# Attention and two feed-forward layers on one core: conversions of weights spread over the steps, the split of x moved to ScalarE and VectorE, the last tiles sent in halves

## The chip, the cores and the metric

The kernel runs on one core of one Trainium2 chip. The metric is the device time of one execution, in microseconds (us). The engines are named as in the profile: PE (TensorE, matmuls) with PEld (its weight loads), DVE (VectorE), ACT (ScalarE), POOL (GpSimd) and SP (SyncE, which here only issues DMAs).

## What is computed

Rotary attention, then a feed-forward layer with g = h - tanh(h), then a gated one without a nonlinearity. All arithmetic of the reference is float32 (the weights reach the chip as 64-bit numbers).

```
attn  = softmax(scale * rot(q) @ rot(k)^T) @ v      # 4 x 8 heads, 576 rows, 64 wide
x     = attn.transpose(0, 2, 1, 3).reshape(2304, 512)
h     = x @ w_in                                    # 512 -> 2048
x2    = (h - tanh(h)) @ w_out                       # 2048 -> 512
a, b  = x2 @ w1, x2 @ w2                            # 512 -> 1024
out   = ((a * b) @ w3) @ w_o2                       # 1024 -> 1024 -> 512
```

## The kernel before

**Precision.** Each operand of a matmul is kept as two parts of a 32-bit type, hi and lo; a product is three matmuls (hi·hi, hi·lo, lo·hi). To *split* a tile is one copy that makes hi and one subtraction that makes lo.

**Stages.** Attention fills the first 296 us, by an order written out as tables of numbers; it is the same before and after. Then the tokens are five blocks of columns: four of 512 and block 4, the *narrow block*, of 256 (the last 64 rows of each of the four sequences). The first feed-forward layer runs in two *halves* of 40 steps (296 to about 750 us): half 0 with hidden columns 0 to 1023, half 1 with the rest, each over the blocks in the order 0, 1, 2, 4, 3, with 8 steps (of 128 hidden columns) per block. Step n issues `emit_h(n+2)` (12 matmuls, x times w_in, L808), `emit_g(n+2)` (g = h - tanh h and its split: ScalarE L821 to L824 and L831, VectorE L825 to L828 and L832), `emit_x2(n)` (12 matmuls into the four x2p accumulators, L846), and then `do(n)`, which performs what a table has put into that step. The last phase (about 750 to 1052 us, `emit_ab` and `emit_out`) makes a·b and multiplies it by w3·w_o2, a product of weights alone.

**Side work in the steps.** The table is filled with `at(step, function)` (L920) and holds, for each half:

- *conversions*: `next_conv` / `to_f32` (L253) turns the next raw 64-bit tile into float32 with two operations on ScalarE (L264, L266) and two on VectorE (L267, L269), and then `next_load` sends SP for another raw tile. The raw pool has two buffers, the z tiles that take the result three. The order of the tiles is the list `units`.
- *placing*: `place` splits a converted tile into its slot (copy on ScalarE L276, subtraction on VectorE L277). A slot is free for the next half's weights only in the last block of the current half (`last`).
- *the folded product*: `conv_o2`, then per 128 rows `wp_trans` (four transposes of w3 on TensorE, and a split) and `wp_mm` (12 matmuls), eight times per half; results go to DRAM (`wp_dram`) and in half 1 come back in a tile `wpe` to be added and split.
- FOLD_AT, FOLD_EVERY, EARLY_EVERY and LATE_EVERY (L177 to L181) say in which steps these stand. EARLY = 4 conversions of the next half's weights are done ahead of its last block, into one tile z_early.

**The split of x.** `split_x` (L774) splits the next block's x on GpSimd, chunk kc by chunk (copy L776, subtraction L777), and stores it to DRAM, whence half 1 loads it (`load_x`, the xl tiles). In half 0 it is called in the last three steps of a block, for the block that follows; at the end of half 1 and in the last phase for x2, the input of that phase (key '3').

**The tail.** After the last block of the last phase two tiles ot of 128x512 are copied from PSUM, one by ScalarE, one by VectorE, and leave in two DMAs each, all issued by SP.

## Time and profile before

| | us |
|---|---|
| median of 3 runs (lowest, highest) | 1060.43 (1058.98, 1061.11) |
| the profiled execution's own time | 1059.08 |
| span of its profile | 1057.3 |
| TensorE busy in it | 1028.3 |
| VectorE, ScalarE, GpSimd busy | 707.9, 610.5, 286.5 |
| mean granted clock of TensorE, of full speed | 0.996 |

The span is what the trace covers of the profiled execution; the execution's own time is 1.8 us longer. A row of a timeline gives the start and the duration of an instruction (or of a run of like ones, xN); in brackets stands the idle time of the engine just before it and what ended it. "L846" is line 846 of the kernel before. A tile's name stands without its number: g, s_out (a slot with w_out), xs (split x), z and raw (converted and raw weights).

### The profile page before, as it was taken

The page shows a single profiled execution, that of the slowest core. Times are in us where ns is not written, and L with a number is a line of the kernel's source. Part 1 is how long each engine was busy: PE and PEld are TensorE (multiplying, and loading weights), DVE is VectorE, ACT ScalarE, POOL GpSimd, SP SyncE. Part 2 cuts the span into 40 slices and gives each one's busy share as a digit, 9 for nine tenths or more (in the row PEclk, how much of TensorE's full clock was granted, in tenths as well). Part 3 has the DMA queues.
Part 4 walks back from the last instruction along what each step waited for, and adds up shares of the span by engine and source line. Part 5 has one row for each costly group of instructions (what it writes and reads, how often), then busy time and mean ns, then how long its engine had stood idle before and what let it go on. Part 6 is the DMA issues. An engine that isn't in the chain of part 4 may idle for free.

```text
span 1057.3 us, 15775 instructions
## 1 busy us (share of the span) xinstructions
PE 1028.3 (97%) x5568; PEld 847.2 (80%) x5568; DVE 707.9 (67%) x1367; ACT 610.5 (58%) x1285; POOL 286.5 (27%) x332
## 2 busy tenths in 40 slices
PE   6989999999999999999999999999999999999998
PEld 5777777777767788888888888898788888888887
DVE  7889999999669866669999776769863212112121
ACT  4779888898767655468888655557652111111111
POOL 3667777777543021111000000040101103020000
PEclk9999999999999999999999999999999999999999
DMA  5658787876444313136335112523630101001010
GB/s 165 158 138 195 180 184 186 185 192 157 88 160 160 100 60 110 40 120 219 108 132 179 60 60 100 168 95 107 239 120 1 40 1 40 1 1 40 1 40 20
DMA packets 71327, 114.99 MB, mean 109 GB/s; under 512 B 12241, under 2 KB 42961, under 8 KB 71249
## 3 DMA queue, kind: packets, MB, share of 16 engines
q1 hardware_dynamic: 71248, 113.99, 37.2%
q8 instruction: 44, 0.72, 0.3%
q14 instruction: 35, 0.28, 0.1%
HBM read 67.96 MB, written 20.45 MB: 84 GB/s over the span
## 4 chain that ended last, share of the span: by engine, by line
PE 82%; DVE 7%; DMA 5%; ACT 3%; issue 2%; POOL 0%; SPq 0%; DVEq 0%; POOLq 0%; ACTq 0%
PE pw L988 19%; PE x2p L846 16%; PE h L808 14%; PE o L1047 9%; PE sc L501 8%; PE pv L597 5%; PE te L556 5%; PE wp L893 4%; DMA qs<-qp 2%; DMA raw_w<-in_moe_w 1%; PE pv L594 1%; PE te L559 1%; DMA q<-in_q 1%; DVE g L832 1%; DMA raw_in<-in_moe_w_in 1%
## 5 line engine op out<-in xcount | busy, mean ns | idle before, releaser
L846 PE MATMUL x2p<-g,s_out 128*128 128x512 f32 (+1 forms) x960 | 216.8, 374 | 7.5 <-DVE g L832 4.6
L846 PEld LDWEIGHTS x2p<-g,s_out 128*128 128x128 f32 x960 | 170.2, 191 | 42.4 <-DVE g L832 7.7
L994 DVE TENSOR_TENSOR ab<-a,pw 128x512 f32<-128x512 f32 (+1 forms) x40 | 25.4, 634 | 173.5 <-PE pw L988 173.5
L528 POOL TENSOR_SCALAR e<-e,r 128x576 f32<-128x576 f32 x144 | 113.4, 799 | 47.4 <-DVE r L524 29.1
L511 ACT ACTIVATE e<-sc,nm 128x576 f32<-128x576 f32 x144 | 107.7, 748 | 28.7 <-DVE nm L506 25.7
L506 DVE TENSOR_REDUCE nm<-sc 128x1 f32<-128x576 f32 x144 | 106.6, 749 | 12.9 <-PE sc L501 11.5
L808 PE MATMUL h<-xl,s_in 128*128 128x512 f32 (+1 forms) x480 | 105.9, 369 | 0.0
L1047 PE MATMUL o<-wpt,abs 128*128 128x512 f32 x432 | 104.5, 390 | 0.0
L808 PEld LDWEIGHTS h<-xl,s_in 128*128 128x128 f32 x480 | 84.0, 188 | 15.2
L501 PE MATMUL sc<-ks,qs 128*128 128x288 f32 x480 | 90.8, 316 | 4.6 <-DMA qs<-qp 3.2
L1047 PEld LDWEIGHTS o<-wpt,abs 128*128 128x128 f32 x432 | 80.6, 188 | 16.4
L825 DVE TENSOR_TENSOR g_s<-g_s,h 128x512 f32<-128x512 f32 (+1 forms) x80 | 50.6, 633 | 59.8 <-ACT g_m L824 59.7
L992 ACT COPY a<-pw 128x512 f32<-128x512 f32 (+1 forms) x40 | 21.7, 543 | 112.8 <-PE pw L988 112.8
L501 PEld LDWEIGHTS sc<-ks,qs 128*128 128x128 f32 x480 | 67.2, 188 | 22.2 <-issue 10.9
L556 PE MATMUL te<-ident,e 128*128 128x128 f32 x576 | 83.8, 277 | 0.6 <-POOL e L528 0.5
L831 ACT CAST g<-g_q 128x512 fp32r<-128x512 f32 (+1 forms) x80 | 46.1, 576 | 51.2 <-DVE g_q L828 50.7
L996 ACT CAST abs<-ab 128x512 fp32r<-128x512 f32 (+1 forms) x40 | 23.1, 577 | 85.5 <-DVE ab L994 85.5
L821 ACT ACTIVATE g_s<-h 128x512 f32<-128x512 f32 (+1 forms) x80 | 44.0, 550 | 49.1 <-PE h L808 48.7
L556 PEld LDWEIGHTS te<-ident,e 128*128 128x128 f32 x576 | 68.8, 143 | 3.5 <-POOL e L528 1.7
L905 POOL TENSOR_TENSOR wpe<-wpe 128x512 fp32r<-128x512 f32 x8 | 10.7, 1335 | 215.4 <-ACT wpe L904 215.4
L832 DVE TENSOR_TENSOR g<-g_q,g 128x512 fp32r<-128x512 f32 (+1 forms) x80 | 55.0, 688 | 19.9 <-ACT g L831 19.5
L828 DVE COPY_PREDICATED g_q<-g_m,g_t 128x512 f32<-128x512 int32 (+1 forms) x80 | 57.0, 713 | 0.9
(299 smaller groups left out, 2119.3 us busy)
## 6 DMA issues: line engine op xcount, KB each, us to landing
ks<-kp SPq DMA_DIRECT2D x60, 288.0 KB, 4.1
raw_w<-in_moe_w SPq DMA_DIRECT2D x32, 512.0 KB, 3.8
raw_in<-in_moe_w_in SPq DMA_DIRECT2D x16, 512.0 KB, 3.8
raw_out<-in_moe_w_out SPq DMA_DIRECT2D x16, 512.0 KB, 3.6
xl<-xs_dram SPq DMA_DIRECT2D x16, 512.0 KB, 5.8
qs<-qp SPq DMA_DIRECT2D x60, 128.0 KB, 3.5
wp_dram<-wpe SPq DMA_DIRECT2D x24, 256.0 KB, 2.0
k<-in_k SPq DMA_DIRECT2D x16, 256.0 KB, 4.2
```

Source lines behind the costliest of these rows:

```text
L501: nc.tensor.matmul(s[:, n, 0:HS], lhs, rhs, start=t == 0, stop=t == len(terms) - 1)
L506: nc.vector.tensor_reduce(d["nm"][:, j:j + 1], d["ss"][j][:, :, 0:HS], AX.XY, ALU.max, negate=True)
L511: nc.scalar.activation(d["e"][:, j, :].rearrange("p (n s) -> p n s", n=2), d["ss"][j][:, :, 0:HS], AF.Exp, bias=d["nm"][:, j:j + 1], accum ...
L528: nc.gpsimd.tensor_scalar(d["e"][:, j, :], d["e"][:, j, :], d["r"][:, j:j + 1], 1.0, ALU.mult, ALU.mult)
L556: nc.tensor.transpose(ps[:, n * 128:(n + 1) * 128], e[:, o + n * 128:o + (n + 1) * 128], ident)
L597: nc.tensor.matmul(ps[64 * j:64 * j + 64, 0:n], vt[:, j, m, :], et[j][:, m, :], start=False, stop=m == NQ - 1, skip_group_check=True)
L808: nc.tensor.matmul(ps[:, 0:w], ws[:, a, kk], x[:, b_, 0:w], start=kc == 0 and t == 0, stop=kc == NK - 1 and t == 2)
L828: nc.vector.copy_predicated(qq, mk.bitcast(I32), t)
L832: nc.vector.tensor_tensor(g[:, 1, 0:w], qq, f32(g[:, 0, 0:w]), ALU.subtract))
L846: nc.tensor.matmul(x2ps[j][o][:, 0:w], ws[:, a, oo], g[:, b_, 0:w], start=c == 0 and t == 0, stop=c == HF - 1 and t == 2)
L988: nc.tensor.matmul(ps[:, 0:w], ws[:, a, kk], x[:, b_, 0:w], start=kc == 0 and t == 0, stop=kc == NK - 1 and t == 2)
L1047: nc.tensor.matmul(outps[j][t], g[:, a, tt], wp[c][:, b_, :], start=c == 0 and i == 0, stop=c == NF2 - 1 and i == 2)
```

## The change

Three things are changed (the three tiles of half 0 that attention leaves unconverted keep their steps 0, 1, 2, though the line that sets them reads otherwise).

1. **Where conversions stand.** `room` gives each step of a half a weight (its block's width, less at the ends of the half) and `spread` deals the conversions of o2 and w3 and the first twelve of the next half's weights evenly over that weight, over blocks 0 to 3 in order (all steps but the last eight). The order of `units` changes with it: the next half's first four stand between the w3 tiles. EARLY is 12 in place of 4: the early tiles wait in x tiles that are no longer read (`early_z`). The last four are converted one step ahead of their placing. In half 1 the tile wpe moves from the buffer of x2 to that of xt (block 4).
2. **split_x** has the copy on ScalarE and the subtraction on VectorE, but for block 0 of half 0 and, in the last phase, blocks 1 to 4, which stay on GpSimd.
3. **The tail**: each of the last two tiles is copied by halves, the left by ScalarE, the right by VectorE, and the second DMA of each is issued by ScalarE.

```diff
-FOLD_AT, FOLD_EVERY = (3, 10), 2.25
-EARLY_EVERY, LATE_EVERY = 2, (0.5, 1)
-EARLY = 4
+CONV_FROM = (2, 1)
+EARLY = 12
...
-    units = half1 + fold[0] + half2 + fold[1] + half3
+    units, work = list(half1), []
+    for i, half in enumerate((half2, half3)):
+        o2u, w3u = fold[i][:NF2 // 2], fold[i][NF2 // 2:]
+        mix = [("o2", r) for r in range(NF2 // 2)]
+        n = 0
+        for f in range(NF2):
+            mix.append(("w3", f))
+            if f < 4:
+                mix.append(("next", n))
+                n += 1
+        mix += [("next", c) for c in range(n, len(half))]
+        work.append(mix)
+        for kd, c in mix:
+            units.append(dict(o2=o2u, w3=w3u, next=half)[kd][c])
...
+    def early_z(hf, i):
+        r, c = divmod(i, 4)
+        if (hf, r) not in early:
+            if hf == 0:
+                early[hf, r] = xpool.tile([128, 4, 512], I32, tag=f"x{r}", name=f"ze0_{r}")
+            elif r == 0:
+                early[hf, r] = xpool.tile([128, 4, 512], I32, tag="x2", name="ze1_0")
+            else:
+                early[hf, r] = xpool.tile([128, 4, 512], I32, tag=f"x{r - 1}", name=f"ze1_{r}")
+        return early[hf, r][:, c]
...
-        nc.gpsimd.tensor_scalar(t[:, 0, 0:w], src[:, kc, :], 1.0, 1.0, ALU.mult, ALU.mult)
-        nc.gpsimd.tensor_tensor(t[:, 1, 0:w], src[:, kc, :], f32(t[:, 0, 0:w]), ALU.subtract)
+        if key[0] == "3" and key[1] or key == (0, 0):
+            nc.gpsimd.tensor_scalar(t[:, 0, 0:w], src[:, kc, :], 1.0, 1.0, ALU.mult, ALU.mult)
+            nc.gpsimd.tensor_tensor(t[:, 1, 0:w], src[:, kc, :], f32(t[:, 0, 0:w]), ALU.subtract)
+        else:
+            nc.scalar.copy(t[:, 0, 0:w], src[:, kc, :])
+            nc.vector.tensor_tensor(t[:, 1, 0:w], src[:, kc, :], f32(t[:, 0, 0:w]), ALU.subtract)
...
-            t = xpool.tile([128, 2, 512], F32, tag="x2", name=f"wpe_{i}{f}")
+            t = xpool.tile([128, 2, 512], F32, tag="xt", name=f"wpe_{i}{f}")
...
+    def room(hf, i):
+        p, c = divmod(i, HF)
+        if hf == 0:
+            r = {0: 0.5, HF - 3: 0.6, HF - 2: 0.6, HF - 1: 0.3}.get(c, 1.0)
+        else:
+            r = {0: 0.5, HF - 1: 0.5}.get(c, 1.0)
+        return r * widths[order[p]] / SM
...
+        n_even = NK + NF2 + EARLY
+        steps = spread(hf, CONV_FROM[hf], H2 - HF, n_even)
+        k = w3_at = 0
+        for m, (kd, c) in enumerate(work[hf]):
+            k = max(k, b0 + steps[m]) if m < n_even else None
+            if kd == "w3":
+                w3_at = k = max(k, w3_at + 1)
+            if kd == "o2":
+                at(k, conv_o2, hf, c)
+            elif kd == "w3":
+                at(k, conv_z, None)
+                at(k + 1, wp_trans, hf, c)
+                at(k + 2, wp_mm, hf, c)
             else:
...
+                if c < EARLY:
+                    at(k, conv_z, lambda hf=hf, c=c: early_z(hf, c))
+                else:
+                    at(last + c // 2 - 1, conv_z, None)
+                at(last + c // 2, place, next_half[c])
...
-                if t % 2:
+                if n == len(seq3) - 1:
+                    nc.scalar.copy(o[:, 0:DM // 2], outps[j][t][:, 0:DM // 2])
+                    nc.vector.tensor_copy(o[:, DM // 2:], outps[j][t][:, DM // 2:])
+                elif t % 2:
...
-                        nc.sync.dma_start(out[bb * S + SM:(bb + 1) * S, :],
-                                          o[64 * r:64 * r + 64, :])
+                        queue = nc.scalar if r else nc.sync
+                        queue.dma_start(out[bb * S + SM:(bb + 1) * S, :],
+                                        o[64 * r:64 * r + 64, :])
```

How the instructions stand on VectorE, at three places. (Line numbers of the changed kernel: L265 and L267 are the conversion, L275 the placing, L805 the subtraction of split_x, L853 to L856 and L860 the chain of g, L884 the addition to x2.)

**First place**: VectorE at the start of half 0, between attention's last row and the first g. Before:

```order
L578 COPY ett1_3_3_4417<-te2_79_4435 128x128
L267 SCALAR_TENSOR_TENSOR z_out6_4582<-z_out6_4582,raw_out6_3738 128x512
L269 SCALAR_TENSOR_TENSOR z_out6_4582<-raw_out6_3738,z_out6_4582 128x512
L267 SCALAR_TENSOR_TENSOR z_in7_4632<-z_in7_4632,raw_in7_4002 128x512
L269 SCALAR_TENSOR_TENSOR z_in7_4632<-raw_in7_4002,z_in7_4632 128x512
L277 TENSOR_TENSOR s_out6_4589<-z_out6_4582,s_out6_4589 128x512
L277 TENSOR_TENSOR s_in7_4639<-z_in7_4632,s_in7_4639 128x512
L825 TENSOR_TENSOR g_s_0_4495<-g_s_0_4495,h_0_4482 128x512
```

After:

```order
L576 COPY ett1_3_3_4417<-te2_79_4435 128x128
L265 SCALAR_TENSOR_TENSOR z_out6_4582<-z_out6_4582,raw_out6_3738 128x512
L267 SCALAR_TENSOR_TENSOR z_out6_4582<-raw_out6_3738,z_out6_4582 128x512
L265 SCALAR_TENSOR_TENSOR z_in7_4632<-z_in7_4632,raw_in7_4002 128x512
L805 TENSOR_TENSOR xs_(0, 1)_0_4730<-x1_1548,xs_(0, 1)_0_4730 128x512
L275 TENSOR_TENSOR s_out6_4589<-z_out6_4582,s_out6_4589 128x512
L267 SCALAR_TENSOR_TENSOR z_in7_4632<-raw_in7_4002,z_in7_4632 128x512
L805 TENSOR_TENSOR xs_(0, 1)_1_4783<-x1_1548,xs_(0, 1)_1_4783 128x512
L853 TENSOR_TENSOR g_s_0_4495<-g_s_0_4495,h_0_4482 128x512
```

The conversions and splits are the same but for the last split (s_in7), which has gone behind the first operations on g; the two subtractions of split_x for block 1 (chunks 0 and 1) stand among them.

**Second place**: VectorE in the narrow block of half 0, step 26's g. Before:

```order
L825 TENSOR_TENSOR g_s_26_5886<-g_s_26_5886,h_26_5873 128x256
L827 TENSOR_TENSOR g_t_26_5888<-h_26_5873,g_t_26_5888 128x256
L826 SCALAR_TENSOR_TENSOR g_q_26_5887<-g_q_26_5887,g_s_26_5886 128x256
L267 SCALAR_TENSOR_TENSOR z_early0_5973<-z_early0_5973,raw_in8_5699 128x512
L828 COPY_PREDICATED g_q_26_5887<-g_m_26_5889,g_t_26_5888 128x256
L269 SCALAR_TENSOR_TENSOR z_early0_5973<-raw_in8_5699,z_early0_5973 128x512
L854 COPY x22_5860<-x2p3_16_5451 128x512
L832 TENSOR_TENSOR g_26_5898<-g_q_26_5887,g_26_5898 128x256
```

After:

```order
L853 TENSOR_TENSOR g_s_26_5952<-g_s_26_5952,h_26_5939 128x256
L855 TENSOR_TENSOR g_t_26_5954<-h_26_5939,g_t_26_5954 128x256
L854 SCALAR_TENSOR_TENSOR g_q_26_5953<-g_q_26_5953,g_s_26_5952 128x256
L856 COPY_PREDICATED g_q_26_5953<-g_m_26_5955,g_t_26_5954 128x256
L860 TENSOR_TENSOR g_26_5964<-g_q_26_5953,g_26_5964 128x256
```

The conversion into z_early and the copy of x2 have left the chain of g, which stands alone.

**Third place**: VectorE in the narrow block of half 1, step 66's g. Before:

```order
L825 TENSOR_TENSOR g_s_66_7939<-g_s_66_7939,h_66_7926 128x256
L827 TENSOR_TENSOR g_t_66_7941<-h_66_7926,g_t_66_7941 128x256
L826 SCALAR_TENSOR_TENSOR g_q_66_7940<-g_q_66_7940,g_s_66_7939 128x256
L881 TENSOR_TENSOR w3t_14_7975<-tw3_14_7970,w3t_14_7975 128x512
L828 COPY_PREDICATED g_q_66_7940<-g_m_66_7942,g_t_66_7941 128x256
L267 SCALAR_TENSOR_TENSOR z_w315_8268<-z_w315_8268,raw_w315_8043 128x512
L269 SCALAR_TENSOR_TENSOR z_w315_8268<-raw_w315_8043,z_w315_8268 128x512
L832 TENSOR_TENSOR g_66_7951<-g_q_66_7940,g_66_7951 128x256
```

After:

```order
L860 TENSOR_TENSOR g_65_8077<-g_q_65_8066,g_65_8077 128x256
L884 TENSOR_TENSOR x22_5934<-x2p3_56_7658,x22_5934 128x512
L265 SCALAR_TENSOR_TENSOR ze1_2_8103<-ze1_2_8103,raw_w14_8004 128x512
L853 TENSOR_TENSOR g_s_66_8123<-g_s_66_8123,h_66_8110 128x256
L267 SCALAR_TENSOR_TENSOR ze1_2_8103<-raw_w14_8004,ze1_2_8103 128x512
L854 SCALAR_TENSOR_TENSOR g_q_66_8124<-g_q_66_8124,g_s_66_8123 128x256
L855 TENSOR_TENSOR g_t_66_8125<-h_66_8110,g_t_66_8125 128x256
L265 SCALAR_TENSOR_TENSOR ze1_2_8103<-ze1_2_8103,raw_w24_8050 128x512
L856 COPY_PREDICATED g_q_66_8124<-g_m_66_8126,g_t_66_8125 128x256
L267 SCALAR_TENSOR_TENSOR ze1_2_8103<-raw_w24_8050,ze1_2_8103 128x512
L860 TENSOR_TENSOR g_66_8135<-g_q_66_8124,g_66_8135 128x256
```

The split of the transposed w3 and the conversion of a w3 tile are gone; two conversions of the last phase's weights into a waiting tile (ze1_2) stand in the chain, and the additions to x2 around it.

## Rows read from the trace of the kernel before

**Rows 1.** The page, part 1: busy us (share of span) xinstructions
```profile
PE 1028.3 (97%) x5568; PEld 847.2 (80%) x5568; DVE 707.9 (67%) x1367; ACT 610.5 (58%) x1285; POOL 286.5 (27%) x332
```

**Rows 2.** Busy us by stretch: PE, PEld, DVE, ACT, POOL; PEclk, DMA share, GB/s
```profile
296.00:350.00 54.00, 48.59 (x194) 38.05 (x193) 48.22 (x65) 39.63 (x70) 17.09 (x14) 0.94 0.46 160
475.00:500.00 25.00, 23.83 (x146) 20.68 (x145) 23.30 (x46) 20.40 (x45) 4.50 (x4) 1.00 0.69 233
500.00:725.00 225.00, 225.00 (x1100) 190.32 (x1099) 182.96 (x304) 152.74 (x282) 19.10 (x16) 1.00 0.33 111
```

**Rows 3.** PE's timeline: start, us, engine line op out<-in xcount [idle <-releaser]
```profile
308.76 4.61 PE L846 MATMUL x2p<-g,s_out 128*128 128x512 f32 x12 [2.01 <-ACT g L831]
...
314.82 2.88 PE L846 MATMUL x2p<-g,s_out 128*128 128x512 f32 x12
...
336.18 0.39 PE L846 MATMUL x2p<-g,s_out 128*128 128x512 f32 x1
337.31 2.81 PE L846 MATMUL x2p<-g,s_out 128*128 128x512 f32 x11 [0.74 <-DVE g L832]
...
343.61 0.51 PE L846 MATMUL x2p<-g,s_out 128*128 128x512 f32 x1 [0.78 <-ACT g L831]
...
345.93 4.38 PE L846 MATMUL x2p<-g,s_out 128*128 128x512 f32 x11 [1.81 <-DVE g L832]
...
483.46 1.58 PE L846 MATMUL x2p<-g,s_out 128*128 128x256 f32 x11 [0.86 <-DVE g L832]
...
748.54 2.83 PE L846 MATMUL x2p<-g,s_out 128*128 128x512 f32 x11 [0.74 <-DVE g L832]
```

**Rows 4.** DVE's timeline, same columns
```profile
300.84 1.66 DVE L269 SCALAR_TENSOR_TENSOR z_in<-raw_in,z_in 128x512 int32<-128x512 int32 x1
302.43 1.78 DVE L277 TENSOR_TENSOR s_out<-z_out,s_out 128x512 fp32r<-128x512 f32 x1
304.13 0.68 DVE L277 TENSOR_TENSOR s_in<-z_in,s_in 128x512 fp32r<-128x512 f32 x1
...
345.19 0.68 DVE L832 TENSOR_TENSOR g<-g_q,g 128x512 fp32r<-128x512 f32 x1
345.79 0.68 DVE L825 TENSOR_TENSOR g_s<-g_s,h 128x512 f32<-128x512 f32 x1
...
483.33 0.41 DVE L825 TENSOR_TENSOR g_s<-g_s,h 128x256 f32<-128x256 f32 x1
483.66 0.41 DVE L827 TENSOR_TENSOR g_t<-h,g_t 128x256 f32<-128x256 f32 x1
```

**Rows 5.** POOL's timeline, the splits of x
```profile
301.92 1.74 POOL L777 TENSOR_TENSOR xs_(0, 1)_1_4774<-x,xs_(0, 1)_1_4774 128x512 fp32r<-128x512 f32 x1
...
335.10 1.61 POOL L777 TENSOR_TENSOR xs_(0, 1)_2_4827<-x,xs_(0, 1)_2_4827 128x512 fp32r<-128x512 f32 x1
...
342.39 1.60 POOL L777 TENSOR_TENSOR xs_(0, 2)_1_5216<-x,xs_(0, 2)_1_5216 128x512 fp32r<-128x512 f32 x1
...
482.09 1.05 POOL L776 TENSOR_SCALAR xs_(0, 3)_3_6146<-x 128x512 fp32r<-128x512 f32 x1
...
746.33 1.61 POOL L777 TENSOR_TENSOR xs_('3', 1)_0_9082<-x,xs_('3', 1)_0_9082 128x512 fp32r<-128x512 f32 x1
```

**Rows 6.** Busy us by stretch, as in rows 2, at the start
```profile
300.00:304.00 4.00, 4.00 (x19) 3.32 (x18) 3.96 (x3) 1.96 (x4) 3.66 (x3) 1.00 0.57 197
304.00:308.00 4.00, 2.75 (x13) 1.94 (x11) 3.38 (x6) 3.54 (x7) 0.00 (x0) 1.00 0.96 331
```

**Rows 7.** ACT's timeline, a conversion
```profile
726.33 0.67 ACT L264 ACTIVATE z_early<-raw_w 128x512 f32<-128x512 f32 x1 [2.29 <-DMA raw_w<-in_moe_w]
```

**Rows 8.** The page, part 6: DMA issues, xcount, KB each, us to landing
```profile
raw_w<-in_moe_w SPq DMA_DIRECT2D x32, 512.0 KB, 3.8
```

**Rows 9.** SP's queue at the end of the program
```profile
1052.00 2.47 SPq L1062 DMA_DIRECT2D out<-ot  x4
```

**Rows 10.** DVE's timeline, the last copy
```profile
1052.09 0.69 DVE L1053 COPY ot<-o 128x512 f32<-128x512 f32 x1 [1.40 <-PE o L1047]
```

More of the change, by code (lines that the diff above doesn't have):

```diff
@@ L770, in x2_tile @@
         return ph2.tile([128, NK, widths[j]], F32, tag=f"x2{j}", name=f"x2{j}", bufs=1)
+    early = {}
+    def early_z(hf, i):
[8 more added lines that the diff above has]
+        return early[hf, r][:, c]
     xs = {}
@@ L928, in fused_kernel, with spread @@
     for i, u in enumerate(left):
-        at(i * 4 // len(left), conv_z, None)
-        at(i * 4 // len(left), place, u)
+        at(i, conv_z, None)
+        at(i, place, u)
+    def room(hf, i):
[5 more added lines that the diff above has]
+        return r * widths[order[p]] / SM
+    def spread(hf, first, stop, count):
+        total = sum(room(hf, i) for i in range(first, stop))
+        steps, got = [], 0.0
+        for i in range(first, stop):
+            got += room(hf, i)
+            while len(steps) < count and (len(steps) + 0.5) * total / count <= got:
+                steps.append(i)
+        return steps + [stop - 1] * (count - len(steps))
@@ L931, in fused_kernel @@
     for hf, next_half in enumerate((half2, half3)):
         b0 = hf * H2
-        n = b0 + FOLD_AT[hf]
-        for r in range(4):
-            at(n + r, conv_o2, hf, r)
-        for f in range(NF2):
-            k = int(n + 4 + f * FOLD_EVERY)
-            at(k, conv_z, None)
-            at(k + 1, wp_trans, hf, f)
-            at(k + 2, wp_mm, hf, f)
-        k0 = k + 3
-        free = []
-        def early_z(r, free=free, hf=hf):
-            if not free:
-                free.append(
-                    ph2.tile([128, EARLY, 512], I32, tag="x23", name="z_early0", bufs=1)
-                    if hf == 0 else
-                    xpool.tile([128, EARLY, 512], I32, tag="x0", name="z_early1"))
-            return free[0][:, r, :]
@@ L953, in fused_kernel @@
-        last = b0 + H2 - HF
-        for i, u in enumerate(next_half):
-            p = k0 + i * EARLY_EVERY
-            if i < EARLY:
-                p = min(p, last + i // 2)
-                at(p, conv_z, lambda i=i, f=early_z: f(i))
-            else:
-                p = max(p, int(last + 1 + (i - EARLY) * LATE_EVERY[hf]))
-                p = min(p, b0 + H2 - 3 + i // 2)
-                at(p, conv_z, None)
-            at(max(p, last + i // 2), place, u)
+        last = b0 + H2 - HF
+        n_even = NK + NF2 + EARLY
```

## The prediction

> **What bounds the kernel now.** I read the page first: TensorE is busy 97% of the span [rows 1]. Time can only come from the few stretches in which TensorE stands still or runs slowly, so the next view is the table of busy time by stretch [rows 2], read for two things: busy time short of the stretch's length, and a granted clock below 1. Before 296 us (attention) both programs issue the same instructions, so I start there. From 296 to 350 TensorE is idle 54.00 - 48.59 = 5.41 us, and the clock is 0.94 of full, which costs another 0.06 x 54 = 3.24 us. From 475 to 500 it is idle 1.17 us. From 500 to 725 it is never idle. Near 748 us one more wait of 0.74 us shows [rows 3]. Visible loss: 8.65 + 1.17 + 0.74 = 10.6 us, and the tail after the last matmul. That is about all a change of order can win.
>
> TensorE's timeline shows what the losses are [rows 3]. Each is an x2p group, the second matmul of the feed-forward, waiting for g: 2.01 us at 308.76, then 0.74, 0.78, 1.81, 0.86, 0.74. After the two long idles (2.01; 0.78 and 1.81, with one matmul between) the clock falls from its upper level (2.4 GHz) to the lower (1.2 GHz): 12 matmuls take 4.61 us where 2.88 is usual, 11 take 4.38 where 2.81 is usual, 1.7 and 1.6 us lost. After 0.74 alone it stays up.
>
> Why is g late? VectorE's timeline [rows 4] has operations of 1.66 and 1.78 us where the same kinds take 0.68 and start 0.60 apart (345.19, 345.79). They lie where GpSimd splits the next block's x, an operation of 1.74 us [rows 5]. DMA traffic is not the cause: in 300 to 304 us, where VectorE is stretched (3 instructions started in 4 us), the DMA share is 0.57; in 304 to 308 it is 0.96 and VectorE's six are short [rows 6]. Each of the six waits of TensorE begins during a GpSimd split or within some 3 us after one: start less idle gives 306.75, 336.57, 342.83, 344.12, 482.60, 747.80; the splits are at 301.92, 335.10, 342.39, 482.09, 746.33.
>
> **The change, part by part.**
>
> *The split of x.* Twenty splits (blocks 1, 2, 4, 3 of the first half and block 0 of the last phase, four each) leave GpSimd; block 0's first four and the later ones of the last phase stay. Each adds one copy on ScalarE and one subtraction on VectorE. Sixteen are 512 wide at 0.60 and four 256 wide at 0.33 (483.33 to 483.66) [rows 4]: 16 x 0.60 + 4 x 0.33 = 10.9 us on VectorE over 450 us; it has 225 - 183 = 42 us free in 500 to 725 alone [rows 2]. That is hidden as long as g stays ahead. What is won is the stretching. At the start VectorE needed 304.13 - 300.84 = 3.3 us from one operation to the second next, where 2 x 0.60 = 1.2 would do: 2.1 us lost [rows 4]. The two added subtractions cost 1.2, and the three conversions ahead of them were stretched too, so about the whole 2.0 us wait closes, and the fallen clock with it. At 336 to 346 the waits of 0.74, 0.78 and 1.81 and the second slow stretch go. I leave 0.75 of the 8.65 us standing (ScalarE still has conversions ahead of its casts of g): **-7.9 us**. Bounds: 0 (if stretching was not the cause) and 8.65.
>
> *Idle is not all of a wait.* Back to back, full-width matmuls start (2.88 - 0.39) / 11 = 0.226 us apart though one lasts 0.39 [rows 3], so each idle stretch hides another 0.16 us. The six waits and two or so shorter ones: 8 x 0.16 = 1.3; I take **-1.2 us**.
>
> *The narrow block of the first half.* Block 4 is 256 wide: a step is 24 matmuls, about 2.9 us (11 in 1.58 [rows 3], less the overlap), and the old order put early conversions into it (order, second place). Per step VectorE's five operations on g are 5 x 0.33 = 1.7 us; with 3 or 4 conversion operations it was 3.5 to 4.1 us, and lagged. The new order has the chain alone there: **-1.1** of 1.17 us. Its conversions now sit in steps 8 to 23, where the folded product (12 wide matmuls of 0.226 us and four transposes a unit, some 3 us) gives TensorE work: counted by the new order, 89 us of VectorE (0.60 per full-width operation) against 109 us of TensorE; before, 65 against 106. Steps 22 and 23 are over (12.2 against 8.3 us), after a lead. **+0.3**, between 0 and 3.
>
> *The narrow block of the second half* is the other way round. Its five folded products have moved ahead, so its TensorE time falls from 36 to 27 us in steps 64 to 71, and some eight conversions have moved in (order, third place). VectorE: 21 full-width operations x 0.60 + 8 x 1.7 = 26.2 us against 26.9. This is the tight place of the new order; it had slack before. **+1.0**, between 0 and 6. Loads bear on it too: ScalarE stands still for 2.29 us when a raw tile has not landed, with the casts of g behind it [rows 7]. A raw tile's buffer goes round in 3.8 (landing, [rows 8]) + 2 x 0.67 [rows 7] + 2 x 0.68 = 6.5 us at least, two buffers give a unit every 3.3 us, and steps 62 to 71 want 10 units in 35.2 us, 3.5 each. On SP these loads are queued between xl loads, which wait for the last h of the block before, and wp_dram stores, which wait for ScalarE and GpSimd; both orders do that, the new one with shorter intervals. The wpe tile, now in block 4's x buffer, still goes round singly.
>
> *Before the last phase.* Placing is 2 splits a step, and the conversions are mostly done by then: about 4.9 us of VectorE per step of 24 x 0.226 = 5.4, where the heaviest steps had 6.1. GpSimd still splits block 1 of the last phase at 746.33 [rows 5]. **-0.5** of 0.74 and its hidden part.
>
> *The tail.* Four issues on SP take 2.47 us, 0.62 each, and the first comes out before VectorE's copy of 0.69 has ended [rows 9, 10]. Now both engines copy half of each tile, and two of the four issues are ScalarE's, behind its copies: the last issue ends at about 1053.6 instead of 1054.47. No row shows ScalarE issuing a DMA; if it costs double, 0.2 is won, if nothing, 1.4. **-0.7**, near the middle, since SP's own 0.62 is the nearest row.
>
> Sum: -7.9 - 1.2 - 1.1 + 0.3 + 1.0 - 0.5 - 0.7 = **-10.1 us**. The profiled execution took 1059.08, so 1049.0; the median of the runs is 1.35 higher, 1060.43, and against it I say **1050.3 us**.
>
> **The rivals.**
>
> *A. The new tight places eat part of it (0.18).* For: 26.2 of 26.9 us leaves nothing for a wait, and in the first half's narrow block 3.5 to 4.1 us per 2.9 did stop TensorE. Against: VectorE and ScalarE work two steps ahead. If the narrow block costs 3 to 6 us and one idle is long enough for the clock to fall (1.7 us), the gain is 2.5 to 6.5: 1054 to 1058.
>
> *B. VectorE's own load makes g late, not GpSimd (0.07).* Then 10.9 us of added operations give back what the stretching cost, the 7.9 and its 1.2 do not come, and the rest of the sum leaves about 1: 1058.5 to 1062. For: VectorE is busy 48.2 of 54 us in 296 to 350 [rows 2]. Against: 0.60 against 1.7 us for the same operation. The Trainium skill (Perfetto Trace Analysis, Optimizing Scalar/DVE Operations) speaks for this rival: GpSimd and VectorE share an SBUF port, so that moving operations between those two "might not help". By that rule the sum would be about -1; no run here shows yet which holds.
>
> *C. Slower: loads hold ScalarE (0.09).* The conversions moved into quick steps are 10 in steps 62 to 71 and 11 in steps 17 to 22. If each makes ScalarE wait 2.29 us as at 726.33 [rows 7], that is 48 us; if each stretch starts with some 8 us of lead (two steps and a third), 32 reach TensorE: 1050 + 32 = 1082. Slower than before it becomes where the waits exceed 10 + 16 us over 21 conversions, 1.24 us each. For: two buffers, and 3.3 us per unit against 3.5 wanted. Against: the wait at 726.33 stopped TensorE by nothing that shows, and from 500 to 725 it is never idle [rows 2].
>
> **How the numbers follow.** My forecast, 1046 to 1054, has 0.66, A 0.18, B 0.07, C 0.09. A measurement here tells about 0.2% (2.1 us) from no change. Faster by more: 0.66 + 0.18 = 0.84; within: B, 0.07; slower: C, 0.09. The range reaches down to 1046 (all visible loss, twice the hidden 1.2 and a tail of 1.4 won) and up to 1058, A's end; about 0.2 is left out, B, C and little below.
>
> **What would show it.** Right: no VectorE operation of 512 columns over 1 us between 300 and 345 us; no 2 us idle and a granted clock of 1.00 in 300 to 350; no idle in the first half's narrow block; in the tail, half-width copies and ScalarE's own DMA issues. The places to look for a new wait are the x2p groups of the second half's narrow block, 45 to 70 us ahead of the last phase. Wrong, if the losses of 300 to 350 stay while GpSimd is idle (B), or if ScalarE waits on raw loads with TensorE idle behind it (C).

## The result, and the profile after

The changed kernel takes 1049.16 us (median of 4 runs, 1048.26 to 1051.33) against 1060.41 of the kernel before (4 runs): ratio 0.9905, 95% interval 0.9884 to 0.9926. Run again on another occasion it took 1050.16 (1048.38 to 1053.82), ratio 0.9916 (0.9887 to 0.9946). So the change makes the kernel faster by 0.8 to 1.0%.

The execution that was profiled took 1051.33 us, the slowest of the four; its span is 1049.5. The page's part 1, after:

```profile
PE 1027.4 (98%) x5568; PEld 847.4 (81%) x5568; DVE 701.3 (67%) x1384; ACT 618.8 (59%) x1310; POOL 245.1 (23%) x292
```

TensorE works as long as before [rows 1] in a span that is 7.8 us shorter; GpSimd has 41 us less to do. The table of busy time by stretch (columns as in [rows 2]), after:

```profile
296.00:350.00 54.00, 53.50 (x238) 42.58 (x235) 48.74 (x79) 46.90 (x85) 2.96 (x3) 1.00 0.46 158
475.00:500.00 25.00, 25.00 (x133) 21.59 (x133) 20.92 (x40) 18.24 (x37) 0.00 (x0) 1.00 0.35 127
500.00:725.00 225.00, 224.08 (x1088) 188.12 (x1087) 184.34 (x310) 159.92 (x298) 12.51 (x8) 1.00 0.37 123
680.00:710.00 30.00, 29.08 (x199) 26.25 (x199) 28.19 (x65) 26.45 (x62) 0.00 (x0) 1.00 0.46 155
725.00:750.00 25.00, 25.00 (x112) 20.71 (x112) 24.04 (x36) 17.43 (x31) 5.03 (x4) 1.00 0.31 117
```

From 296 to 350 the idle time has fallen from 5.41 to 0.50 us, and the granted clock there is 1.00. The stretch from 475 to 500 is full. But 500 to 725, full before, now has 0.92 us of idle, all of it between 680 and 710, where VectorE is busy 28.19 of 30 us. The waits that TensorE's timeline marks between attention and the last phase, after:

```profile
323.37 2.83 PE L874 MATMUL x2p<-g,s_out 128*128 128x512 f32 x11 [0.33 <-DVE g L860]
...
442.43 2.58 PE L921 MATMUL wp<-o,w3t 128*128 128x512 f32 x10 [0.24 <-DVE w3t L909]
...
456.85 0.50 PE L874 MATMUL x2p<-g,s_out 128*128 128x512 f32 x1 [0.79 <-ACT g L859]
457.58 2.77 PE L874 MATMUL x2p<-g,s_out 128*128 128x512 f32 x11 [0.23 <-DVE g L860]
...
680.90 2.79 PE L874 MATMUL x2p<-g,s_out 128*128 128x512 f32 x11 [0.20 <-DVE g L860]
...
685.98 0.62 PE L874 MATMUL x2p<-g,s_out 128*128 128x256 f32 x3 [0.49 <-DVE x L884]
...
695.41 1.34 PE L874 MATMUL x2p<-g,s_out 128*128 128x256 f32 x9 [0.15 <-DVE g L860]
```

Against [rows 3] the waits of 2.01 and 1.81 us are gone, and with them the slow clock. In their place stand small ones, the largest of 0.79 and 0.49, at the end of block 2 of half 0 and around the narrow block of half 1. VectorE's timeline at the start of half 0, after:

```profile
300.75 0.68 DVE L805 TENSOR_TENSOR xs_(0, 1)_0_4730<-x,xs_(0, 1)_0_4730 128x512 fp32r<-128x512 f32 x1
301.35 0.68 DVE L275 TENSOR_TENSOR s_out<-z_out,s_out 128x512 fp32r<-128x512 f32 x1
301.95 0.68 DVE L267 SCALAR_TENSOR_TENSOR z_in<-raw_in,z_in 128x512 int32<-128x512 int32 x1
302.56 0.68 DVE L805 TENSOR_TENSOR xs_(0, 1)_1_4783<-x,xs_(0, 1)_1_4783 128x512 fp32r<-128x512 f32 x1
```

These are the operations of [rows 4] that took 1.66 and 1.78 us, now 0.68, with the subtractions of split_x (L805) among them. Where GpSimd still splits, VectorE is still held:

```profile
740.58 1.78 DVE L275 TENSOR_TENSOR s_w<-ze,s_w 128x512 fp32r<-128x512 f32 x1
...
743.33 1.78 DVE L275 TENSOR_TENSOR s_w<-z_w,s_w 128x512 fp32r<-128x512 f32 x1
```

but TensorE has no wait near 740.

**Lost start time.** Idle time hides a part of each wait, so I also summed for every profile, over the matmuls after attention, the time from one start to the next less that of a full queue (0.227 us for 512 columns, 0.120 for 256, 0.088 for a transpose). The sections are: the first 60 us of the feed-forward; from there to the end of the narrow block of half 0; from there to 10 us before the narrow block of half 1; that block with these 10 us; the last block of half 1. "Tail" is the time from the end of the last matmul to the end of the span; "start" is when the first h matmul begins. All in us, from one profile each; the tail is good to about 0.05, since the span is read to 0.1. Each ratio is to runs of the kernel before on the same chip, where its medians lay between 1057.62 and 1060.41; so medians of different rows are compared by their ratios:

| kernel | median | ratio to before (95%) | start | first 60 us | rest of half 0 | to half 1's narrow block | that block | last block | sum | tail |
|---|---|---|---|---|---|---|---|---|---|---|
| before | 1060.41 | | 296.1 | 10.5 | 3.2 | 1.0 | 0.5 | 1.8 | 17.2 | 5.25 |
| the change | 1049.16 | 0.9905 (0.9884 to 0.9926) | 296.9 | 2.1 | 3.2 | 1.1 | 2.5 | 0.1 | 9.1 | 4.81 |
| the change again | 1050.16 | 0.9916 (0.9887 to 0.9946) | 294.7 | 2.2 | 3.0 | 1.1 | 2.8 | 0.1 | 9.4 | 4.95 |
| split alone | 1052.16 | 0.9921 (0.9891 to 0.9950) | 297.5 | 3.6 | 2.3 | 0.4 | 0.5 | 3.6 | 10.6 | 5.19 |
| split undone | 1064.73 | 1.0043 (1.0024 to 1.0062) | 294.9 | 10.6 | 3.2 | 2.1 | 3.7 | 0.7 | 20.5 | 4.86 |
| extra work on GpSimd | 1062.10 | 1.0029 (1.0014 to 1.0043) | 295.6 | 11.7 | 4.9 | 1.2 | 3.8 | 0.1 | 21.9 | 4.85 |
| stores by GpSimd | 1051.82 | 0.9936 (0.9911 to 0.9962) | 295.1 | 2.0 | 1.3 | 2.9 | 5.1 | 0.1 | 11.5 | 5.02 |
| narrow block freed | 1053.43 | 0.9947 (0.9926 to 0.9968) | 300.1 | 2.2 | 2.7 | 1.1 | 3.5 | 0.0 | 9.6 | 5.00 |
| both | 1057.31 | 0.9990 (0.9974 to 1.0005) | 298.3 | 1.5 | 1.0 | 4.0 | 7.1 | 0.0 | 13.8 | 4.99 |
| tail with whole tiles | 1047.72 (1 run) | | 294.1 | 2.2 | 2.6 | 1.1 | 2.5 | 0.1 | 8.5 | 4.63 |
| half 0's stores, whole tiles | 1049.92 | 0.9931 (0.9905 to 0.9956) | 295.5 | 2.2 | 1.4 | 1.1 | 2.1 | 0.1 | 7.0 | 4.82 |
| xl loads spread | 1050.07 (1 run) | | 294.8 | 3.0 | 3.2 | 1.1 | 2.4 | 0.1 | 9.9 | 4.96 |
| these three | 1050.34 | 0.9935 (0.9912 to 0.9958) | 297.2 | 2.7 | 3.0 | 1.1 | 2.6 | 0.1 | 9.6 | 4.74 |
| three raw tiles | 1048.11 | 0.9894 (0.9871 to 0.9917) | 295.1 | 1.8 | 2.7 | 1.4 | 1.5 | 0.0 | 7.5 | 4.97 |

In the two profiles of the change the loss is 8.1 and 7.8 us smaller than before and the tail 0.4 and 0.3, together 8.5 and 8.1 us. The medians moved by 11.3 and 8.9 us, with intervals (7.8 to 12.3, 5.7 to 12.0) that hold both sums. What the medians have beyond the sums was not located; the column "start" differs by 6 us between profiles of programs that issue the same attention. Differences below 2 us are therefore read from the lost start time, and the medians serve as a check.

### The profile page after: what moved, and what is told of

Read it like the earlier page. It is cut to its first block, busy times and chain, and to the rows that moved or that the text cites. A ratio compares the mean times of both kernels' runs of the same rounds, so it can differ in the third digit from the quotient of the medians.

```text
span 1049.5 us, 15763 instructions
## 1 busy us (share of the span) xinstructions
PE 1027.4 (98%) x5568; PEld 847.4 (81%) x5568; DVE 701.3 (67%) x1384; ACT 618.8 (59%) x1310; POOL 245.1 (23%) x292
## 4 chain that ended last, share of the span: by engine, by line
PE 78%; DVE 8%; DMA 6%; ACT 5%; issue 2%; SPq 0%; POOL 0%; ACTq 0%; DVEq 0%; POOLq 0%
PE pw L1025 19%; PE h L836 12%; PE x2p L874 12%; PE o L1084 9%; PE sc L499 9%; PE pv L595 6%; PE te L554 6%; DMA raw_w<-in_moe_w 2%; PE wp L921 2%; PE pv L592 1%; DMA raw_in<-in_moe_w_in 1%; PE te L557 1%; DVE g L860 1%; DMA raw_out<-in_moe_w_out 1%; DMA ks<-kp 1%
## 5 line engine op out<-in xcount | busy, mean ns | idle before, releaser
L874 PE MATMUL x2p<-g,s_out 128*128 128x512 f32 (+1 forms) x960 | 213.5, 370 | 2.4 <-DVE g L860 0.9
L504 DVE TENSOR_REDUCE nm<-sc 128x1 f32<-128x576 f32 x144 | 106.6, 749 | 12.7 <-PE sc L499 11.5
L853 DVE TENSOR_TENSOR g_s<-g_s,h 128x512 f32<-128x512 f32 (+1 forms) x80 | 50.5, 631 | 40.2 <-ACT g_m L852 40.2
L859 ACT CAST g<-g_q 128x512 fp32r<-128x512 f32 (+1 forms) x80 | 46.1, 577 | 33.2 <-DVE g_q L856 32.7
L860 DVE TENSOR_TENSOR g<-g_q,g 128x512 fp32r<-128x512 f32 (+1 forms) x80 | 50.8, 635 | 17.6 <-ACT g L859 16.6
L856 DVE COPY_PREDICATED g_q<-g_m,g_t 128x512 f32<-128x512 int32 (+1 forms) x80 | 56.0, 700 | 0.8
```

Of the source, the lines that this page charges most:

```text
L504: nc.vector.tensor_reduce(d["nm"][:, j:j + 1], d["ss"][j][:, :, 0:HS], AX.XY, ALU.max, negate=True)
L856: nc.vector.copy_predicated(qq, mk.bitcast(I32), t)
L860: nc.vector.tensor_tensor(g[:, 1, 0:w], qq, f32(g[:, 0, 0:w]), ALU.subtract))
L874: nc.tensor.matmul(x2ps[j][o][:, 0:w], ws[:, a, oo], g[:, b_, 0:w], start=c == 0 and t == 0, stop=c == HF - 1 and t == 2)
```

## The experiments

**1. The split of x alone.** The kernel before with the new split_x:

```diff
+        if key[0] == "3" and key[1] or key == (0, 0):
...
+        else:
+            nc.scalar.copy(t[:, 0, 0:w], src[:, kc, :])
+            nc.vector.tensor_tensor(t[:, 1, 0:w], src[:, kc, :], f32(t[:, 0, 0:w]), ALU.subtract)
```

> The kernel before with one edit: the split of x on ScalarE and VectorE as in the change, nothing else moved. Theory 1 (GpSimd's splits stretch VectorE's operations and make g late): 1051 to 1054 us; the losses of 300 to 350 us go but for about 1 us, granted clock 1.00 there, no VectorE operation of 512 columns over 1.2 us between 300 and 345; the wait of 0.7 us near 748 stays, since those splits stay on GpSimd. Theory 2 (VectorE's own load makes g late, the change's gain is from moving the conversions): 1060 to 1062 us, VectorE operations short but TensorE still waiting 4 us or more in 300 to 350.

1052.16 us (5 runs), ratio 0.9921: within its interval all of the change's gain. Its busy time in 296 to 350 us, and TensorE's timeline before the last phase:

```profile
296.00:350.00 54.00, 52.49 (x233) 41.08 (x230) 46.37 (x75) 44.66 (x81) 3.60 (x4) 1.00 0.44 154
```

```profile
736.10 0.49 PE L850 MATMUL x2p<-g,s_out 128*128 128x512 f32 x1 [0.92 <-ACT g L835]
...
743.34 2.79 PE L850 MATMUL x2p<-g,s_out 128*128 128x512 f32 x11 [0.74 <-DVE g L836]
```

The idle time of the first stretch is 1.51 us, the clock 1.00. Theory 1 holds for it, theory 2 (rival B) falls. The last block of half 1, however, lost 3.6 us in this profile (the slowest of the five runs), before 1.8: the old order's conversions stand there, and one of them kept ScalarE waiting for a raw tile:

```profile
721.24 0.67 ACT L264 ACTIVATE z_early<-raw_w 128x512 f32<-128x512 f32 x1 [4.38 <-DMA raw_w<-in_moe_w]
```

**2. The split undone.** The changed kernel with split_x on GpSimd throughout (the edit above, reversed).

> The changed kernel with the split of x back on GpSimd, conversions and tail as in the change. Theory 1: 1056 to 1059 us, the waits of 300 to 350 us are back with the low clock. Theory 2: 1048 to 1050.5 us.

1064.73 us (10 runs): not only slower than the change, but slower than the kernel before, by 0.24 to 0.62%. Busy time of 296 to 350, and TensorE's timeline:

```profile
296.00:350.00 54.00, 48.67 (x196) 38.37 (x195) 49.79 (x67) 39.94 (x70) 15.80 (x13) 0.94 0.46 159
```

```profile
307.46 4.61 PE L870 MATMUL x2p<-g,s_out 128*128 128x512 f32 x12 [1.98 <-ACT g L855]
...
344.62 4.37 PE L870 MATMUL x2p<-g,s_out 128*128 128x512 f32 x11 [1.83 <-DVE g L856]
...
718.39 1.59 PE L870 MATMUL x2p<-g,s_out 128*128 128x256 f32 x11 [0.70 <-DVE g L856]
```

The two long waits and the slow matmuls behind them (4.61 and 4.37 us) are back, in their old sizes [rows 3]. And the conversions' new places cost 3.7 us in the narrow block of half 1, where they had cost 0.5: with GpSimd splitting, the moved conversions by themselves are a loss. That cost is in none of theory 1's numbers, and the run came out above them.

**3. GpSimd busy with nothing.** The changed kernel, and GpSimd does a copy and a subtraction beside each split, whose result nobody reads:

```diff
+            d = ph2.tile([128, SM // 2], F32, tag="extra", name=f"extra_{key}_{kc}", bufs=1)
+            for c in range(0, w, SM // 2):
+                nc.gpsimd.tensor_scalar(d, src[:, kc, c:c + SM // 2], 1.0, 1.0, ALU.mult, ALU.mult)
+                nc.gpsimd.tensor_tensor(d, src[:, kc, c:c + SM // 2], d, ALU.subtract)
```

> The changed kernel, and beside each split of x on ScalarE and VectorE GpSimd does a copy and a subtraction of the same width (in pieces of 256 columns) into a tile that nobody reads. Theory 1, in its strong form (GpSimd's work of itself holds VectorE up, whoever needs its result): 1054 to 1060 us, VectorE operations over 1.2 us again in 298 to 345. If instead what cost time was that the split's result came late from a slow engine: 1048 to 1051 us.

1062.10 us (10 runs). Busy time of 296 to 350, VectorE's and TensorE's timelines:

```profile
296.00:350.00 54.00, 47.27 (x190) 35.68 (x190) 52.63 (x64) 42.02 (x74) 49.38 (x57) 0.97 0.37 128
```

```profile
300.83 1.22 DVE L275 TENSOR_TENSOR s_out<-z_out,s_out 128x512 fp32r<-128x512 f32 x1
...
302.78 1.23 DVE L805 TENSOR_TENSOR xs_(0, 1)_1_4788<-x,xs_(0, 1)_1_4788 128x512 fp32r<-128x512 f32 x1
```

```profile
307.35 0.96 PE L878 MATMUL x2p<-g,s_out 128*128 128x512 f32 x3 [1.41 <-ACT g L863]
...
321.21 3.63 PE L878 MATMUL x2p<-g,s_out 128*128 128x512 f32 x9 [1.43 <-DVE g L864]
```

GpSimd's timeline beside the two rows of VectorE:

```profile
300.46 1.05 POOL L809 TENSOR_TENSOR extra_(0, 1)_0_4733<-x,extra_(0, 1)_0_4733 128x256 f32<-128x256 f32 x1
...
302.40 1.06 POOL L809 TENSOR_TENSOR extra_(0, 1)_1_4791<-x,extra_(0, 1)_1_4791 128x256 f32<-128x256 f32 x1
```

Many of VectorE's operations take 0.88 or 1.2 us for 0.68, it is busy 52.63 of 54 us, and 9.6 us of start time are lost anew in the first 60 us, more than theory 1 had. Not all are stretched: the first three operations on g (L857 to L859) stay at 0.67 or 0.68 throughout the stretch. Every stretched one ends just after an operation of GpSimd: the two here at 302.05 and 304.01, where GpSimd's end at 301.51 and 303.46, and all over 0.8 us between 297 and 350 us end 0.53 to 0.62 us after one. In the kernel before the same holds for all over 1 us after 297 us (0.54 to 0.61). So VectorE's operation waits until GpSimd's has ended. This settles that GpSimd's work of itself holds VectorE, whoever needs its result. (It is a larger dose than the splits of before: since nothing waits for it, GpSimd runs through in one piece, 49 us against the 17 of [rows 2].) The Trainium skill (SBUF — State Buffer, Who interferes with whom) calls the port pair that the two engines share an exclusive lock. The traces agree with a wait for GpSimd's operation to end: 0.68 us becomes up to 1.2 beside GpSimd's operations of 256 columns here, and up to 1.78 beside those of 512 [rows 4, 5], where the end again comes 0.55 us after GpSimd's (304.21 after 303.66).

**4. The changed kernel again**, for a second profile.

> The changed kernel once more, for a second profile of it: 1048 to 1051.5 us. If the losses of TensorE around 442 to 458 and 680 to 706 us come from the order, they stand in this profile at the same steps; if they come from single late loads, they differ.

The losses stand at the same places with nearly the same sizes (table), so what is left comes from the order and not from chance. The chain of waits of the first profile names it, in the steps before both places (start, us, what):

```profile
435.14 3.67 DMA raw_in<-in_moe_w_in
...
440.53 0.53 ACT g L859
...
443.73 3.66 DMA raw_in<-in_moe_w_in
...
449.10 0.52 ACT g L859
...
450.24 0.52 ACT xs_(0, 3)_0_6104 L804
...
454.88 0.60 DVE xs_(0, 3)_1_6148 L805
...
670.89 5.95 DMA raw_w<-in_moe_w
...
679.50 0.63 ACT g L859
```

ScalarE's cast of g (L859) stands behind a conversion, which stands behind the load of a raw tile; and such a load takes 3.7 us at 435 and 443 but 5.95 at 670, where four xl loads run beside it (landing in 6.4 us, median from 660 to 690). Before the wait of 0.79 us at 456.85 the chain also runs through split_x itself: three copies on ScalarE (449.62 to 450.76) and a subtraction on VectorE (454.88), 1.74 us of work that the change has put there. The next runs try the loads (theory L) against the plain amount of work (theory W).

**5. The stores of the folded product by GpSimd**, **6. the narrow block of half 1 freed of conversions**, and **7. both**:

```diff
-            nc.sync.dma_start(wp_dram[rows, 0], t)
+            nc.gpsimd.dma_start(wp_dram[rows, 0], t)
...
-            nc.sync.dma_start(wp_dram[rows, 0], t[:, 1, :])
-            nc.sync.dma_start(wp_dram[rows, 1], t[:, 0, :])
+            nc.gpsimd.dma_start(wp_dram[rows, 0], t[:, 1, :])
+            nc.gpsimd.dma_start(wp_dram[rows, 1], t[:, 0, :])
...
-            r = {0: 0.5, HF - 1: 0.5}.get(c, 1.0)
+            r = {0: 0.5, HF - 1: 0.5}.get(c, 1.0) if p < 3 else 0.0
```

> The changed kernel with the stores of the folded product issued by GpSimd instead of SP, so that the raw load behind a store on SP no longer waits for ScalarE's copy. Theory L (late raw loads cause what is left of TensorE's losses, 2.2 to 2.5 us in 425 to 475 and 2.6 to 2.9 in 675 to 725): both fall to about 1 us, ScalarE's waits on raw loads there fall, 2 to 4 us less after 296 us. Theory W (too much work of VectorE and ScalarE in those steps, the loads only fill the waiting): within 0.7 us of the changed kernel. Third: GpSimd's issues of themselves stretch VectorE, and it is slower.

> The changed kernel with no conversions dealt to the narrow block of half 1 (its weight is 0 in room; the same 24 conversions stand in the steps before it). Theory W: the loss of 2.6 to 2.9 us in 675 to 725 falls to under 1, and no new one over 1 us comes in 500 to 675, since TensorE's folded product gives time there: 1.5 to 2.5 us less. Theory L: the loads come closer together in the steps before, and the loss moves there: within 0.7 us.

> Both edits, stores by GpSimd and no conversions in the narrow block of half 1. If the two causes are separate, their gains add, 3 to 5 us under the changed kernel after 296 us; if they are one, it equals the better of the two.

Run 5 has the change of queue, 6 that of room, 7 both. The stores' edit does in half 0 what theory L says (3.2 to 1.3 us) and the opposite in half 1 (1.1 to 2.9 before the narrow block, 2.5 to 5.1 in it). There, ScalarE's and TensorE's timelines:

```profile
679.09 0.66 ACT L262 ACTIVATE ze<-raw_w 128x512 f32<-128x512 f32 x1 [3.65 <-DMA raw_w<-in_moe_w]
```

```profile
680.31 0.50 PE L874 MATMUL x2p<-g,s_out 128*128 128x512 f32 x1 [1.87 <-ACT g L859]
...
681.03 4.34 PE L874 MATMUL x2p<-g,s_out 128*128 128x512 f32 x11 [0.22 <-DVE g L860]
```

one raw tile comes 3.65 us late (its load at 672.06 takes 7.01 us), and after TensorE's wait of 1.87 the clock falls (11 matmuls in 4.34 us; granted 0.72 of full from 680 to 686). Why it is late there, whether from a store that lands later or from the other order that SP's queue took, was not separated. The third possibility, that GpSimd's issues stretch VectorE, does not show: between 350 and 720 us three of VectorE's operations of 512 columns take over 0.95 us, as many as in the change's first profile.

Freeing the narrow block (6) did not help either: 3.5 us for 2.5 to 2.8 in that section. That the conversions and their loads now come closer before the block is the likely reason, and not shown. In sum it is within 0.5 us of the change (theory L had 0.7); what its median has beyond that is not in the lost start time, and its profile has the latest start of all, 300.1. ScalarE and TensorE:

```profile
683.52 0.66 ACT L262 ACTIVATE ze<-raw_w 128x512 f32<-128x512 f32 x1 [2.56 <-DMA raw_w<-in_moe_w]
```

```profile
685.28 0.49 PE L874 MATMUL x2p<-g,s_out 128*128 128x512 f32 x1 [2.01 <-ACT g L859]
```

This wait is as long as the first of [rows 3], but the clock stays up: the 11 matmuls after it take 2.81 us, and the granted clock is 1.00 from 683 to 690. So the length of the wait alone does not tell whether the clock falls; what else decides was not tested.

Together (7) they are worse than either, 7.1 us, and a gain over the kernel before is no longer shown (ratio 0.9990, 0.9974 to 1.0005). In all three profiles a late raw tile stands before TensorE's longest wait.

**8. The tail with whole tiles.** One tile copied by ScalarE, one by VectorE, as before; the second DMA of each still on ScalarE's queue.

```diff
-                    nc.scalar.copy(o[:, 0:DM // 2], outps[j][t][:, 0:DM // 2])
-                    nc.vector.tensor_copy(o[:, DM // 2:], outps[j][t][:, DM // 2:])
+                    (nc.vector.tensor_copy if t else nc.scalar.copy)(o, outps[j][t])
```

> The changed kernel, the last two tiles copied whole again (one by ScalarE, one by VectorE), the second DMA of each still issued by ScalarE. From the end of the last matmul to the end of the span: the changed kernel takes 4.8 to 4.95 us, the kernel before 5.25. If the gain is that of two queues, 4.7 to 4.95 here; if it is that of the halves, 5.1 to 5.3. The halves run one after another in the changed kernel (VectorE waits for ScalarE's), so I expect the first.

4.63 us, a little under the range for two queues. The changed kernel's tail, in ScalarE's, VectorE's and SP's timelines, and its DMA issues (engine, count, KB each, us to landing):

```profile
1044.05 0.37 ACT L1090 COPY ot<-o 128x256 f32<-128x256 f32 x1 [1.16 <-PE o L1084]
1044.73 0.37 ACT L1090 COPY ot<-o 128x256 f32<-128x256 f32 x1 [0.31 <-PE o L1084]
1044.91 1.46 ACTq L1103 DMA_DIRECT2D out<-ot  x2
```

```profile
1044.45 0.42 DVE L1091 COPY ot<-o 128x256 f32<-128x256 f32 x1 [1.10 <-ACT ot L1090]
1045.13 0.42 DVE L1091 COPY ot<-o 128x256 f32<-128x256 f32 x1 [0.26 <-ACT ot L1090]
```

```profile
1044.91 1.19 SPq L1103 DMA_DIRECT2D out<-ot  x2
```

```profile
out<-ot SPq DMA_DIRECT2D x2, 128.0 KB, 2.4
out<-ot ACTq DMA_DIRECT2D x2, 128.0 KB, 2.8
```

VectorE's half waits each time for ScalarE's half of the same tile (1044.05 + 0.37, then 1044.45), so the halves save nothing (whether the wait is for the shared tile ot or for the shared PSUM tile was not separated); the two queues do, and the run without halves keeps their gain. Over all profiles with two queues: nine with halves, 4.81 to 5.02 us; three with whole tiles, 4.63 to 4.82.

**9. Half 0's stores by GpSimd and whole tiles; 10. xl loads one a step; 11. all three.**

```diff
-            if c2 == 1 and nblk <= p2 + 1 < 2 * nblk:
+            if 1 <= c2 <= NK and nblk <= p2 + 1 < 2 * nblk:
...
-                for kc in range(NK):
-                    load_x((1, j3), j3, kc, widths[j3])
+                load_x((1, j3), j3, c2 - 1, widths[j3])
```

> The changed kernel with two edits: the stores of the folded product in half 0 alone by GpSimd (half 1's stay on SP), and the last two tiles copied whole. From the earlier profiles: TensorE's loss in 425 to 475 us falls from 2.2 to 2.5 to about 0.6 us, that in 675 to 725 stays at 2.6 to 2.9, the tail takes 4.6 to 4.7. After attention about 1.9 us less than the changed kernel: 1046 to 1049 us.

> The changed kernel with the four xl loads of half 1 issued one a step, not four in one step. Theory D (the raw loads before the narrow block of half 1 land in about 6 us instead of 3.8 because xl loads stand before them on SP and beside them in the DMA engines): the loss in 675 to 725 falls from 2.6 to 2.9 to 1.5 us or less and raw_w loads around 668 land in under 5 us. Theory W (VectorE has too much to do there): loss 2.4 us or more, as before.

> All three edits. If theory D holds: about 1.2 us under the run with two edits, 1045 to 1048 us. If W: equal to it.

With two edits the lost start time is 7.0 us, 2 less than the change's, but the ratio of 7 runs (0.9931) is not below the change's. Spreading the xl loads left the narrow block at 2.4, in one run: theory D got no support from it. The raw load there still took 5.82 us (at 669.67), so the edit did not bring about the early landing that D asks for, and that xl loads are what makes it slow is not shown. With all three, the gain in half 0 was absent from the profile (3.0). A version that is faster than the change was not shown by these.

**12. Three raw tiles**, taken from the xs tiles:

```diff
-Z_BUFS, X_BUFS, E_BUFS = 3, 6, 4
+Z_BUFS, X_BUFS, E_BUFS = 3, 5, 4
...
-        raw = conv.tile([128, 512], I64, tag="raw", name=f"raw_{kind}{i}")
+        raw = conv.tile([128, 512], I64, tag="raw", name=f"raw_{kind}{i}", bufs=3)
```

> The changed kernel with three raw tiles in place of two; the room comes from the xs tiles, five in place of six. Theory L (with two buffers a raw load starts only when a conversion has ended, and ScalarE waits for it): ScalarE's waits on raw loads of 1 to 3 us in 430 to 450 and at 668 to 685 go, TensorE's losses in 425 to 475 (2.2 to 2.5) and 675 to 725 (2.6 to 2.9) fall under 1 us each: 1045 to 1048 us, if five xs tiles are enough. Theory W (work of VectorE and ScalarE): the losses stay at 2 us or more with the loads on time. If five xs tiles are too few, new waits of h on xs show at the ends of blocks.

1048.11 us (1046.86 to 1048.87, 4 runs), ratio 0.9894. The narrow block of half 1 loses 1.5 us for 2.5 to 2.8, the rest of half 0 hardly less. Busy time of 680 to 710 and TensorE's wait there:

```profile
680.00:710.00 30.00, 29.14 (x207) 27.28 (x206) 29.42 (x67) 26.37 (x62) 0.00 (x0) 1.00 0.42 141
```

```profile
683.65 0.62 PE L874 MATMUL x2p<-g,s_out 128*128 128x256 f32 x3 [0.86 <-DVE x L884]
```

VectorE is now busy 29.42 of 30 us, and the wait left is for its addition to x2 (L884). But the waits on raw tiles that theory L wanted gone are not all gone: ScalarE still waits 3.16 us at 437.85, 2.96 at 445.22 and 2.37 at 674.63, and the load behind the last still takes 6.24 us; gone is the one of 0.92 at 684.59. So neither theory holds as it stands. That the microsecond won in that block was raw tiles coming late is likely, and not shown: the edit also took an xs tile away. The wait that is left is VectorE's work. The sum of losses is 1.6 to 1.9 us under the change's, and the median 1.1 to 2.1; the intervals of the ratios overlap, so it may be the fastest of all, and is not shown to be.

## Why the prediction was right, and where its terms were off

The forecast was 1050.3 us, 1046 to 1058; 1049.16 and 1050.16 were measured. Its main step, that GpSimd's splits stretch VectorE and the late g then costs TensorE its clock as well, stood up to three runs that could have felled it (1, 2, 3). Rival B fell with run 1: VectorE's and ScalarE's added operations cost nothing that shows in 296 to 350 us (at 449 to 455 they stand in a chain that ends in a wait, experiment 4). The Trainium skill (Perfetto Trace Analysis, Optimizing Scalar/DVE Operations) warns that moving work between GpSimd and VectorE "might not help". Read as rival B reads it, run 1 should have been at 1060 or more; it was at 1052, so here it did help, and the sharing that the page gives as its reason speaks for the main step, not for B.

That 1049.16 and 1050.16 came so near to 1050.3 is in part luck. The forecast's terms add up to -10.1; the lost start time and the tail show -8.5 and -8.1, the terms below missed in both directions, and the medians had a part that was not located.

Term by term, against the lost start time:

- *The split of x*, -7.9, with its part of the hidden -1.2: 10.5 to 2.1 or 2.2, so -8.4 or -8.3. Right; the split alone (run 1) brings 6.9 of it, and without the split (run 2) none comes. None of VectorE's operations of 512 columns between 300 and 345 us is longer than 0.78 in the change's two profiles.
- *The narrow block of half 0*, -1.1 and +0.3: the net is 0 or -0.2 (3.2 to 3.2 or 3.0). The waits in the block did go, but the step "over in steps 22 and 23, after a lead: +0.3" was mis-sized: at the end of block 2 new waits of the same total came (442.43 to 457.58 above).
- *The narrow block of half 1*, +1.0: +2.0 and +2.3. Named rightly as the tight place, sized at half. It is rival A's mechanism at less than A's price (3 to 6 us): the granted clock stayed at 1.00 (680 to 710).
- *Before the last phase*, -0.5: -1.7. I took GpSimd's splits at 746 as what would remain; they still stretch VectorE (740.58, 743.33 above), but two of the three operations over 1 us there are now placings (L275), and TensorE does not wait. With the old conversions in that block the last operation on g takes 1.78 us right before the wait of 0.74, at 746.70 in the kernel before and at 741.51 in run 1. Run 1 loses 3.6 there; run 2, with the moved conversions and all splits on GpSimd, 0.7. So it is the moved conversions that removed the loss, and GpSimd had its part in it.
- *The tail*, -0.7: -0.4 and -0.3. Two queues brought the last issue forward about as reckoned: it ends 1.68 us after the last matmul (1046.37 - 1044.69), before 2.42 (1054.47 [rows 9] - 1052.05). But the DMAs on ScalarE's queue landed after 2.8 us, those on SP's after 2.4, which gave 0.4 back. The two issues on ScalarE take 0.56 and 0.78 us, those on SP 0.54 and 0.51 (the 1.46 and 1.19 above hold the wait for the second tile's copy as well).

Rival C's mechanism exists too. For six of the seven raw tiles that it converts between 423 and 448 us ScalarE waits 1.2 to 1.6 us, about the 1.24 us from which C was to decide:

```profile
425.44 0.69 ACT L262 ACTIVATE ze<-raw_out 128x512 f32<-128x512 f32 x1 [1.16 <-DMA raw_out<-in_moe_w_out]
...
438.84 0.67 ACT L262 ACTIVATE z_in<-raw_in 128x512 f32<-128x512 f32 x1 [1.55 <-DMA raw_in<-in_moe_w_in]
...
447.41 0.68 ACT L262 ACTIVATE z_in<-raw_in 128x512 f32<-128x512 f32 x1 [1.50 <-DMA raw_in<-in_moe_w_in]
```

By C's working, 11 conversions at 1.24 us, less 8 of lead, would have cost TensorE 5.6 us in that stretch; all of the rest of half 0 lost 3.2. The step that failed in C is most likely the lead, which it lets be spent once: ScalarE is busy 36.6 of the 50 us from 425 to 475 (second profile of the change), so it has slack there to earn lead again. No run tried this by itself.

So the gain is the split's, but for 0.3 to 0.4 us of the tail; the conversions' part is of two signs. On top of the new split they gain 1.2 to 1.5 us by the lost start time (10.6 to 9.1 or 9.4; from a single profile of run 1, and not separable in the medians), under the old one they lose 3.3 (17.2 to 20.5), and there the medians agree.

## What to carry to other kernels

An engine with idle time can still be what costs: before work is left on GpSimd because it is free there, look in VectorE's timeline for operations that take longer than their kind beside it. Price an edit by the runs with and without its neighbours: the moved conversions were worth about +1 or -3 us, depending on who split x. And when the total moves by some microseconds, locate the time by start-to-start sums per stage, since run-to-run differences in another stage can be as large.

## What was not expected

- The attention, the same in all programs, ended between 294.1 and 300.1 us in 14 profiles, more than most of the effects studied.
- Two copies into two halves of one tile, on two engines, ran one after the other (1044.05 to 1044.42, then from 1044.45).
- Late raw tiles made ScalarE wait 1.2 to 1.6 us in six of seven conversions, and little of it reached TensorE.
- A wait of TensorE of 2.01 us was followed by the slow clock in the kernel before and not in run 6.
